# A dense layer worked as seven products: VectorE's and ScalarE's work in a pair of tiles put in another order, and the next tokens' columns prepared one step per pair

## The chip, the cores and the metric

The kernel runs on one core of a Trainium2 chip. The metric is the device time of one execution in microseconds (us). Three executions were timed, and one more was profiled; the rows below come from that one.

## The reference, cut to what matters

Three layers follow each other: attention, a routed layer that sends each token to one of eight experts, and a dense layer. The change touches the dense layer alone, and the hand-over to it.

```python
def _moe2_ref(x, w_in, w_out):          # x: 1792 x 768, w_in: 768 x 2048, w_out: 2048 x 768
    h = x @ w_in
    alpha = 1.0
    g = np.where(h > 0.0, h, alpha * (np.exp(np.minimum(h, 0.0)) - 1.0))
    return (g @ w_out).astype(np.float32)
```

## The kernel before, in words

All products are in 32-bit precision, made of rounded operands: a matrix `w` is split into a high part (a ScalarE cast) and a low part (a VectorE subtraction, `w` minus the high part), and a product takes three matmuls: high by high, high by low, low by high. `split` does this (L1440 the cast, L1441 the subtraction), for columns of `w_in` and for rows of `w_out`.

The 1792 tokens of the dense layer are 14 tiles of 128, worked in four blocks: blocks 0, 1 and 2 of four tiles (512 tokens), block 3 of two. The 2048 middle features are 16 tiles `f` of 128. Blocks 0 and 3 take one `f` at a time: `up` (18 matmuls over 512 or 256 tokens, L1487 to L1489), the curve (`curve`), and later `down`, which adds the tile's share to the output sums: for each of the token tiles six matmuls (L1519), three into 512 and three into 256 columns.

Blocks 1 and 2 take the features in eight pairs (`pair_step`) and get the pair's two `up` products from seven smaller ones instead of eight (`part(o, w, x, i)`, nine matmuls each over 256 tokens, L1540 to L1544). Here they are called P0 to P6 by their `i`; the order on TensorE is P1, P0, P3, P6, P2, P5, P4. They need, ready ahead of time:

- seven prepared forms of the tokens' columns, high and low (`x7`). For the next block they are made during this one: `rows_in` fetches a tile of rows, `columns_in` transposes it on TensorE (three matmuls for each of two halves, L145) and lets ScalarE copy it to a work buffer (L1376), `plain` makes the first three forms and then the four differences (L1395), `mixed` the other four forms (L1387, L1388).
- prepared forms of the pair's `w_in` columns: `a1` (P1, P0), `ss` (P3, P6, P2, P5) and `a2` (P4), split anew for the pair after this one while this one runs; and `sums` (L1463 to L1466, four VectorE operations) for the pair after that.

There are two PSUM banks for the parts, X and Y, each of 512 columns. P1 writes the right half of X, P0, P6, P5 and P4 the left half, P3 and P2 the left half of Y. Between them ScalarE copies (`p1`, `u2`, `p5`) and VectorE adds (L1599, L1612, L1614) put the pair's two products `h[0]` and `h[1]` together in SBUF. P6 may start when L1599 has read X.

The curve is, for a 128x512 tile: two ScalarE activations (L1496, L1497), a VectorE operation that gives `m` (L1498), a ScalarE cast `gh` (L1501) and a VectorE subtraction `gl` (L1502). `down` for feature tile `f` needs `gh`, `gl` and the split rows of `w_out`, `woh` and `wol`. In blocks 1 and 2 the `down` of a pair runs within the next pair: here D0 to D3 are its four token tiles for the pair's even feature tile, and E0 to E3 those for the odd one. After a block's last tile `finish` copies the output sums to the buffers `raw_t` (L1552), and POOL scatters them to the output (L1556).

The order of TensorE's, VectorE's and ScalarE's instructions is that of the code: each of the three works its list strictly one after the other. DMA loads of `w_in` and `w_out` (`refill`) are issued by SyncE's queue, which keeps up to five of each ahead.

Of the kernel before, what the change touches and what calls it, by code (L numbers as in the profile page):

```python
# [23 lines left out]
P = 128  # L24
# [70 lines left out]
def build(nc, tc, a):  # L95
# [3 lines left out]
    with ExitStack() as top:  # L99
# [1210 lines left out]
        with ExitStack() as st:  # L1310
# [20 lines left out]

            xr_t = [four(b0p.tile([P, WCH], F32, name="xr0")), four(raw_t[1])]

# [32 lines left out]
            def columns_in(bi, k, g, nxt, bank):  # L1366

                if not 0 <= k < blocks[bi][1]:
                    return
                t, r = turn_of(bi, k), rows_tile(k)  # L1370
                pt = bank.rearrange("p (c n) -> p c n", c=4)[:, :3]
                for j in range(3):
                    cc = 3 * g + j
                    flip(pt[:, j], r[:, cc * P : (cc + 1) * P])
                if seven[bi]:
                    nc.scalar.copy(xr_t[bi > 1][:, 2 * (t // 2) + g], pt)  # L1376
                    if (t // 2, g) == (1, 1):
                        plain(bi, nxt, t % 2)
                    return
                xh, xl = nxt  # L1380
                o = (slice(None), slice(3 * g, 3 * g + 3), slice(t * P, (t + 1) * P))
                nc.scalar.copy(xh[o], pt)
                nc.vector.tensor_sub(xl[o], pt, xh[o])
# [6 lines left out]
            def plain(bi, nxt, t):  # L1390
                r = xr_t[bi > 1]
                halves_in(nxt, slice(0, 2), r[:, :2], t)
                halves_in(nxt, slice(2, 3), r[:, 3:], t)
                for o, m, n in ((0, 2, 0), (2, 3, 2), (3, 3, 0), (1, 1, 3)):
                    nc.vector.tensor_sub(r[:, o], r[:, m], r[:, n])  # L1395

            def mixed(bi, nxt, t):
                r = xr_t[bi > 1]
                for o in (slice(0, 2), slice(2, 4)):
                    halves_in(nxt, slice(o.start + 3, o.stop + 3), r[:, o], t)  # L1400
# [90 lines left out]

            def curve(n, ph):
                m = gp.tile([P, TB * P], F32, name="m", bufs=1)
                gh = gp.tile([P, TB * P], F32R, name="gh")
                gl = gp.tile([P, TB * P], F32R, name="gl")
                nc.scalar.activation(m[:, :n], ph[:, :n], AF.Relu, scale=-1.0)  # L1496
                nc.scalar.activation(m[:, :n], m[:, :n], AF.Exp, scale=-1.0)  # L1497
                nc.vector.scalar_tensor_tensor(  # L1498
                    m[:, :n], m[:, :n], -1.0, ph[:, :n], op0=ALU.add, op1=ALU.max
                )  # L1500
                nc.scalar.copy(gh[:, :n], m[:, :n])  # L1501
                nc.vector.tensor_sub(gl[:, :n], m[:, :n], gh[:, :n])  # L1502
                return gh, gl

            def regions(acc, t):
# [77 lines left out]

            def pair_step(bi, p, x, pend, nxt):
                n = TB * P
# [13 lines left out]
                nc.vector.tensor_add(h[0][:, :HT], xr, p1)  # L1599
                if pairs:  # L1600
                    split_first(*after)
                    w_next = None
# [34 lines left out]

# [8 lines left out]
            nxt = None  # L1646
            pend = []
            for bi, (t0, nt) in enumerate(blocks):
                ahead_ = bi + 1 < len(blocks)
                if seven[bi]:  # L1650
                    for p in range(KF2 // 2):
                        if p == 3:
# [6 lines left out]
                        pend, w_in = pair_step(bi, p, xs, pend, nxt)  # L1659
                    xs = nxt  # L1660
                    continue
                for f in range(KF2):
# [11 lines left out]
                    ph = up(nt * P, [xs], *w_in) if bi or f else acc_t[1]  # L1674
                    w_in = w_next
                    if f + 1 == KF2 and ahead_:
                        split_sums(0)
                        split_sums(1)
                        split_last(bi + 1, 0)
                    g = curve(nt * P, ph)  # L1680
                    if ahead_:
                        turn, half = divmod(f - 6, 2)
                        if half == 0:
                            rows_in(bi + 1, turn)
                        turn, half = divmod(f - 7, 2)
                        if f == 7:
                            nxt = x_tiles(bi + 1)
                        if turn in (2, 4) and half == 0:
                            mixed(bi + 1, nxt, turn // 2 - 1)
                        if turn >= 0:  # L1690
                            columns_in(bi + 1, turn, half, nxt, next(halfway))
                    if bi == 0:
                        w2 = split_out(bi, f)
                    if due:
                        narrow_wide(due, 1)
                    if w2 is None:
                        run_down(pend[:TB])
                        pend = pend[TB:]
                        w2 = split_out(bi, f)
# [49 lines left out]
```

## Time and profile before

| | |
|---|---|
| three timed executions | 937.79, 938.77 (median), 940.61 us |
| the profiled execution's own time | 939.29 us |
| its span, first to last instruction | 937.5 us |
| attention and routed layer | 0 to about 403 us |
| dense layer, block 0 | about 403 to 546.3 us |
| blocks 1 and 2 (the pairs) | 546.3 to 856.4 us |
| block 3 and the last stores | 856.4 to 937.5 us |

The borders are read from TensorE's instructions: the first part at 546.29 us, the first `up` matmul of block 3 at 856.41 us. The span and the 1.8 us around it make the profiled execution's own time, which is 0.5 us above the median.

### The profile page before, as it was taken

How to read it: one execution, taken by the hardware profiler on the slowest of the kernel's cores; microseconds unless marked ns; L12 is line 12 of the kernel's file. 1: busy time of each engine (PE TensorE's matmuls, PEld its weight loads, DVE VectorE, ACT ScalarE, POOL GpSimd, SP SyncE). 2: the span in 40 equal slices, each digit the busy share in tenths (PEclk: the TensorE clock that was granted, in tenths of full speed). 3: DMA queues.
4: the chain of work that ended last, by engine and by line, in shares of the span. 5: the costliest groups of instructions: out<-in, count | busy, mean ns of one | idle time of the engine just before them, and what ended most of it. 6: DMA issues, size and time to landing. Idle time of an engine off the chain costs nothing.

```text
span 937.5 us, 15343 instructions
## 1 busy us (share of the span) xinstructions
PE 869.8 (93%) x5620; PEld 728.5 (78%) x5620; DVE 641.2 (68%) x1036; ACT 524.6 (56%) x796; POOL 82.2 (9%) x79
## 2 busy tenths in 40 slices
PE   9899999999998989999999976998888898999998
PEld 5444555989997878888887776887878788889997
DVE  5778786975664658858888876666565666564664
ACT  7677765534554548645455544554445455554664
POOL 1000001122010124510000001000000100000100
PEclk9999999999999999999999997999889999999999
DMA  9798867899461769478654734232222333223640
GB/s 326 260 320 310 306 232 253 290 400 378 168 237 56 269 245 398 155 265 275 208 159 127 265 105 148 85 119 85 85 85 68 134 103 101 73 97 100 237 153 34
DMA packets 64203, 180.83 MB, mean 193 GB/s; under 512 B 8010, under 2 KB 12234, under 8 KB 64098
## 3 DMA queue, kind: packets, MB, share of 16 engines
q1 hardware_dynamic: 59474, 160.27, 49.8%
q0 software_dynamic: 4480, 19.01, 5.9%
q8 instruction: 59, 0.97, 0.4%
q14 instruction: 46, 0.38, 0.1%
q10 hardware_dynamic: 144, 0.20, 0.1%
HBM read 152.58 MB, written 29.89 MB: 195 GB/s over the span
## 4 chain that ended last, share of the span: by engine, by line
PE 33%; DVE 12%; ACT 9%; issue 3%; DVEq 0%; ACTq 0%
PE acc L1519 7%; PE pt L1519 7%; PE acc L1540 3%; PE acc L1544 3%; PE acc L1543 3%; PE acc L1487 3%; PE acc L1489 3%; PE acc L1488 3%; DVE m L1498 2%; DVE wol L1441 2%; ACT m L1497 2%; ACT gh L1501 2%; ACT m L1496 2%; ACT woh L1440 1%; DVE wi L1464 1%
## 5 line engine op out<-in xcount | busy, mean ns | idle before, releaser
L594 DVE TENSOR_TENSOR wlo<-raw,whi 128x1536 fp32r<-128x1536 f32 x64 | 111.6, 1761 | 31.3 <-ACT whi L592 26.1
L253 ACT ACTIVATE at<-ps,bias 128x896 f32<-128x896 f32 x96 | 82.6, 916 | 39.1 <-PE ps L300 36.1
L592 ACT CAST whi<-raw 128x1536 fp32r<-128x1536 f32 x64 | 93.7, 1480 | 15.4 <-PE acc L603 9.0
L1519 PE MATMUL acc<-wol,gh 128*128 128x256 f32 x320 | 101.0, 316 | 0.0
L1519 PE MATMUL acc<-woh,gh 128*128 128x256 f32 x320 | 100.9, 315 | 0.0
L1519 PE MATMUL acc<-woh,gl 128*128 128x256 f32 x320 | 100.6, 314 | 0.0
L1540 PE MATMUL acc<-x,ss 128*128 128x256 f32 x192 | 61.6, 321 | 40.3 <-DVE h L1599 40.3
L601 PE MATMUL acc<-whi,both 128*128 128x384 f32 (+1 forms) x236 | 85.1, 361 | 4.3 <-issue 2.7
L602 PE MATMUL acc<-wlo,both 128*128 128x384 f32 (+1 forms) x236 | 83.4, 354 | 0.6 <-DVE wlo L594 0.6
L603 PE MATMUL acc<-whi,both 128*128 128x384 f32 (+1 forms) x236 | 83.2, 352 | 0.0
L1540 PEld LDWEIGHTS acc<-x,ss 128*128 128x128 f32 x192 | 42.4, 221 | 43.4 <-DVE h L1599 43.3
L1501 ACT CAST gh<-m 128x512 fp32r<-128x512 f32 (+1 forms) x64 | 36.3, 567 | 59.6 <-DVE m L1498 59.6
L1519 PEld LDWEIGHTS acc<-woh,gh 128*128 128x128 f32 x320 | 60.3, 188 | 10.1
L1502 DVE TENSOR_TENSOR gl<-m,gh 128x512 fp32r<-128x512 f32 (+1 forms) x64 | 40.0, 626 | 40.5 <-ACT gh L1501 39.8
L1519 PEld LDWEIGHTS acc<-wol,gh 128*128 128x128 f32 x320 | 60.3, 188 | 9.3
L1441 DVE TENSOR_TENSOR wol<-wor,woh 128x768 fp32r<-128x768 f32 x64 | 61.0, 954 | 7.9 <-ACT woh L1440 7.1
L1441 DVE TENSOR_TENSOR a<-wir,a 128x768 fp32r<-128x768 f32 (+1 forms) x47 | 38.4, 817 | 37.3 <-ACT a L1440 36.7
L1519 PEld LDWEIGHTS acc<-woh,gl 128*128 128x128 f32 x320 | 60.1, 188 | 4.3
L274 PE MATMUL po<-at,vt 128*64 128x448 f32 (+1 forms) x300 | 59.4, 532 | 2.4 <-DVE xT L305 2.4
L1543 PE MATMUL acc<-x,ss 128*128 128x256 f32 x192 | 59.2, 308 | 0.0
L1544 PE MATMUL acc<-x,ss 128*128 128x256 f32 x192 | 59.0, 307 | 0.0
L1440 ACT CAST woh<-wor 128x768 fp32r<-128x768 f32 x64 | 53.3, 833 | 2.8 <-PE acc L1519 2.8
(325 smaller groups left out, 2337.9 us busy)
## 6 DMA issues: line engine op xcount, KB each, us to landing
raw<-in_w SPq DMA_DIRECT2D x132, 384.0 KB
wor<-wo_d SPq DMA_DIRECT2D x60, 384.0 KB
wir<-wi_d SPq DMA_DIRECT2D x58, 384.0 KB
raw<-in_wi SPq DMA_DIRECT2D x9, 768.0 KB
raw<-in_wo SPq DMA_DIRECT2D x9, 768.0 KB
raw<-in_wi SPq DMA_DIRECT2D x14, 384.0 KB
raw<-in_wo SPq DMA_DIRECT2D x14, 384.0 KB
qr<-in_q SPq DMA_DIRECT2D x11, 448.0 KB
```

The costliest lines, as they stand in the source:

```text
L253: nc.scalar.activation(out, ps, AF.Sigmoid, bias=bias, scale=QK_SCALE)
L592: nc.scalar.copy(w_hi, raw)
L594: nc.vector.tensor_sub(w_lo, raw, w_hi)
L601: nc.tensor.matmul(o, a_hi, b_hi, start=first, stop=False)
L602: nc.tensor.matmul(o, a_hi, b_lo, start=False, stop=False)
L603: nc.tensor.matmul(o, a_lo, b_hi, start=False, stop=last)
L1440: nc.scalar.copy(pair[0], raw)
L1441: nc.vector.tensor_sub(pair[1], raw, pair[0])
L1519: nc.tensor.matmul(o, a, b, start=(clears and f == 0 and k_ == 0), stop=(f == KF2 - 1 and k_ == 2), skip_group_check=True,)
L1540: nc.tensor.matmul(o, a, b, start=(start and cc == 0), stop=False, skip_group_check=True)
L1543: nc.tensor.matmul(o, a, c, start=False, stop=False, skip_group_check=True)
L1544: nc.tensor.matmul(o, al[:, cc], b, start=False, stop=(cc == 2), skip_group_check=True)
```

## The change

No instruction of VectorE, ScalarE or TensorE in these blocks is added or taken away: the lists are put in another order, and one work buffer becomes two for block 2's columns.

1. The curve is cut into `rise` (to `m`) and `parts_of` (`gh`, `gl`). In a pair, the curve of `h[0]` now comes right behind the adds that make it, and ahead of P4; that of `h[1]` right behind P4's copy.
2. `sums`, which came at the end of a pair, now comes in the middle, behind the curve of `h[0]`.
3. The split of the odd `w_out` rows, which ended a pair, is put off to the middle of the next pair (`late`).
4. On TensorE, D0 now runs between P3 and P6, then D1 and D2, P4, D3 and E0 to E3. Before, D0 and D1 stood behind P5, then P4 and the other six.
5. The next tokens' columns: in blocks 1 and 2 the transposes come at pairs 1 to 4 (before: 3 to 6), and `plain`, `differences` and `mixed` are steps of their own at the end of pairs 2 to 7, one a pair (before: `plain` with the differences in pairs 4 and 6, `mixed` in pairs 5 and 7). For block 2 the work buffers are `raw_t[1]` and `raw_t[0]`, in place of `raw_t[1]` alone.
6. In block 0 the columns are made at feature tiles 3 to 6 and 10 to 13 (before: 7 to 14), and the steps at 7, 8, 9, 13, 14 and 15 (before: 10, 11, 14 and 15). At the last feature tile, the preparation of the first pair moves behind the curve.

```diff
-            xr_t = [four(b0p.tile([P, WCH], F32, name="xr0")), four(raw_t[1])]
+            xr_t = [[four(b0p.tile([P, WCH], F32, name="xr0"))] * 2, [four(raw_t[j]) for j in (1, 0)]]
...
-                    nc.scalar.copy(xr_t[bi > 1][:, 2 * (t // 2) + g], pt)
-                    if (t // 2, g) == (1, 1):
-                        plain(bi, nxt, t % 2)
+                    nc.scalar.copy(xr_t[bi > 1][t % 2][:, 2 * (t // 2) + g], pt)
...
-            def pair_step(bi, p, x, pend, nxt):
+            def pair_step(bi, p, x, pend, late, nxt):
...
-                rows_in(bi + 1, p - 2)
+                rows_in(bi + 1, p)
...
                 part(yl, w_s[0], x, 3, True)
                 nc.scalar.copy(p5, yl)
+                run_down(pend[:1])
                 part(xl, w_s[1], x, 6)
...
                 nc.vector.tensor_add(h[1][:, HT:], xl, p5)
+                m0 = rise(n, h[0])
                 if pairs:
                     split_sums(1)
-                run_down(pend[:2])
+                g0 = parts_of(n, m0)
+                pend2 = late() if late else []
+                if pairs and seven[later_[0]]:
+                    sums(*later_)
+                run_down(pend[1:3])
                 part(xl, a2, x, 4)
                 nc.scalar.copy(h[1][:, :HT], xl)
                 if pairs:
                     split_last(*after)
-                k = p - 3
-                if seven[bi + 1] and p in (5, 7):
-                    mixed(bi + 1, nxt, (p - 5) // 2)
-                columns_in(bi + 1, k, 0, nxt, Y)
-                g0 = curve(n, h[0])
-                run_down(pend[2:4])
-                columns_in(bi + 1, k, 1, nxt, X)
+                columns_in(bi + 1, p - 1, 0, nxt, Y)
+                m1 = rise(n, h[1])
+                run_down(pend[3:])
+                columns_in(bi + 1, p - 1, 1, nxt, X)
                 w20 = split_out(bi, 2 * p)
-                g1 = curve(n, h[1])
-                run_down(pend[4:])
-                if pairs and seven[later_[0]]:
-                    sums(*later_)
-                w21 = split_out(bi, 2 * p + 1)
+                g1 = parts_of(n, m1)
+                run_down(pend2)
+                if seven[bi + 1]:
+                    for j, todo in enumerate((plain, differences, mixed)):
+                        for t in range(2):
+                            if p == 2 + 3 * t + j:
+                                todo(bi + 1, nxt, t)
                 refill()
-                return tiles_of(bi, 2 * p, g0, w20) + tiles_of(bi, 2 * p + 1, g1, w21), w_next
+
+                def rest_of():
+                    return tiles_of(bi, 2 * p + 1, g1, split_out(bi, 2 * p + 1))
+
+                return tiles_of(bi, 2 * p, g0, w20), rest_of, w_next
```

Three places show what moved. The first is VectorE's list in a pair of block 2, before, from the split of `a2` to the add that opens the next pair (L1599). `h_15291` and `h_15292` are `h[0]` and `h[1]`, `acc_1907` is X, `a_11803` the low part of `a2`; `wi_1827` and `sraw` take the sums.

```order
L1441 TENSOR_TENSOR a_11803<-wir,a_11802 128x384
L1498 SCALAR_TENSOR_TENSOR m<-m,h_15291 128x512
L1502 TENSOR_TENSOR gl<-m,gh 128x512
L1441 TENSOR_TENSOR wol<-wor,woh 128x768
L1498 SCALAR_TENSOR_TENSOR m<-m,h_15292 128x512
L1502 TENSOR_TENSOR gl<-m,gh 128x512
L1463 TENSOR_TENSOR wi_1827<-wir 128x384
L1464 TENSOR_TENSOR wi_1827<-wi_1827,wir 128x384
L1465 TENSOR_TENSOR sraw<-wir,wi_1827 128x384
L1466 TENSOR_TENSOR sraw<-wir 128x384
L1441 TENSOR_TENSOR wol<-wor,woh 128x768
L1599 TENSOR_TENSOR h_15458<-acc_1907,p_15460 128x256
```

The same engine and stretch in the changed kernel, from the low part of the last `ss` to the add that opens the next pair, which is L1606 there.

```order
L1442 TENSOR_TENSOR ss_11805<-sraw,ss_11804 128x768
L1506 TENSOR_TENSOR gl<-m,gh 128x512
L1442 TENSOR_TENSOR wol<-wor,woh 128x768
L1464 TENSOR_TENSOR wi_1827<-wir 128x384
L1465 TENSOR_TENSOR wi_1827<-wi_1827,wir 128x384
L1466 TENSOR_TENSOR sraw<-wir,wi_1827 128x384
L1467 TENSOR_TENSOR sraw<-wir 128x384
L1442 TENSOR_TENSOR a_11803<-wir,a_11802 128x384
L1497 SCALAR_TENSOR_TENSOR m<-m,h_15286 128x512
L1442 TENSOR_TENSOR wol<-wor,woh 128x768
L1506 TENSOR_TENSOR gl<-m,gh 128x512
L1606 TENSOR_TENSOR h_15452<-acc_1907,p_15454 128x256
```

The four sums and the odd `wol` stood right ahead of the next pair's first add; now they stand in the middle of the pair, ahead of `m` of `h[1]`, and between the pair's last `gl` and that add nothing is left.

The second place is TensorE's matmuls from P3 to P6 in a pair of block 2, before (`acc_1908` is Y, `acc_1907` X).

```order
L1540 MATMUL acc_1908<-x_13524,ss_11804 128x256
L1543 MATMUL acc_1908<-x_13525,ss_11804 128x256
L1544 MATMUL acc_1908<-x_13524,ss_11805 128x256
L1540 MATMUL acc_1907<-x_13524,ss_11804 128x256
L1543 MATMUL acc_1907<-x_13525,ss_11804 128x256
L1544 MATMUL acc_1907<-x_13524,ss_11805 128x256
```

The same place in the changed kernel; `pt_1905` and `acc_1911` are the output sums of token tile 0.

```order
L1550 MATMUL acc_1908<-x_13185,ss_11804 128x256
L1551 MATMUL acc_1908<-x_13184,ss_11805 128x256
L1526 MATMUL pt_1905<-woh,gh 128x512
L1526 MATMUL pt_1905<-wol,gh 128x512
L1526 MATMUL pt_1905<-woh,gl 128x512
L1526 MATMUL acc_1911<-woh,gh 128x256
L1526 MATMUL acc_1911<-wol,gh 128x256
L1526 MATMUL acc_1911<-woh,gl 128x256
L1547 MATMUL acc_1907<-x_13184,ss_11804 128x256
L1550 MATMUL acc_1907<-x_13185,ss_11804 128x256
```

D0, six matmuls, now stands between the last matmul of P3 and the first of P6.

The third place is ScalarE's list at the first half-column of block 2 that is copied to the work buffer (`raw_121` is `raw_t[1]`; what an instruction waits for stands behind it, DMASW4 being one of POOL's transfers). Before, in pair 3 of block 1:

```order
L1619 COPY h_13527<-acc_1907 128x256 [waits PE_49]
L1440 CAST a_11802<-wir 128x384 [waits DMAHW1_49]
L1376 COPY raw_121<-acc_1908 128x384 [waits DMASW4_49,DVE_49,PE_49]
L1496 ACTIVATE m<-h_13526 128x512 [waits Activation_49]
L1497 ACTIVATE m<-m 128x512 [waits Activation_49]
L1501 CAST gh<-m 128x512 [waits DVE_49]
```

In the changed kernel, in pair 1 of block 1:

```order
L1632 COPY h_13187<-acc_1907 128x256 [waits PE_49]
L1441 CAST a_11802<-wir 128x384 [waits DMAHW2_49]
L1376 COPY raw_121<-acc_1908 128x384 [waits DMASW4_49,PE_49]
L1495 ACTIVATE m<-h_13187 128x512 [waits DVE_49,Activation_49]
L1496 ACTIVATE m<-m 128x512 [waits Activation_49]
L1376 COPY raw_121<-acc_1907 128x384 [waits PE_49]
L1441 CAST woh<-wor 128x768 [waits DMAHW7_49]
L1505 CAST gh<-m 128x512 [waits DVE_49]
```

The copy waits for the same transfer, two pairs sooner, and `h[1]`'s curve and the split of `woh` stand behind it on the engine.

## Rows read from the trace of the kernel before

**Rows 1.** Busy PE, PEld, DVE, ACT, POOL; PEclk; DMA share, GB/s; blocks 1 and 2.

```profile
546.30:856.40 310.10, 269.81 (x1788) 250.37 (x1789) 190.90 (x295) 158.75 (x284) 10.49 (x10) 0.94 0.30 96
```

**Rows 2.** Waits of TensorE, 400 to 938 us: total, times, longest.

```profile
PE acc L1540 <- DVE h L1599: 40.3, 15, 7.4
PE acc L1540 <- DVE m L1498: 3.4, 1, 3.4
...
PE acc L1487 <- DVE m L1498: 1.3, 2, 0.9
PE pt L1519 <- DVE wol L1441: 1.1, 1, 1.1
```

**Rows 3.** Timeline of TensorE over one pair: start, duration, instruction, idle before.

```profile
592.32 0.38 PE L1540 MATMUL acc<-x,ss 128*128 128x256 f32 x1 [1.40 <-DVE h L1599]
...
597.75 0.28 PE L1540 MATMUL acc<-x,a 128*128 128x256 f32 x1
...
598.83 0.40 PE L1519 MATMUL acc<-woh,gh 128*128 128x512 f32 x1
...
599.88 0.40 PE L1519 MATMUL acc<-woh,gh 128*128 128x512 f32 x1
...
608.25 0.28 PE L1544 MATMUL acc<-x,ss 128*128 128x256 f32 x1
609.92 0.38 PE L1540 MATMUL acc<-x,ss 128*128 128x256 f32 x1 [1.39 <-DVE h L1599]
```

**Rows 4.** Timeline of TensorE after the longest wait.

```profile
572.27 0.58 PE L1540 MATMUL acc<-x,ss 128*128 128x256 f32 x1 [7.40 <-DVE h L1599]
...
577.56 0.41 PE L1540 MATMUL acc<-x,ss 128*128 128x256 f32 x1
```

**Rows 5.** Timeline of VectorE at the same pair's end.

```profile
606.46 0.55 DVE L1463 TENSOR_TENSOR wi<-wir 128x384 f32<-128x384 f32 x1
...
608.58 0.95 DVE L1441 TENSOR_TENSOR wol<-wor,woh 128x768 fp32r<-128x768 f32 x1
609.45 0.42 DVE L1599 TENSOR_TENSOR h<-acc,p 128x256 f32<-128x256 f32 x1
```

**Rows 6.** Timeline of ScalarE at that place.

```profile
607.49 0.37 ACT L1598 COPY p<-acc 128x256 f32<-128x256 f32 x1 [0.94 <-PE acc L1544]
```

**Rows 7.** VectorE's groups by shape, 546 to 856 us: total, mean ns, idle before.

```profile
L1441 DVE TENSOR_TENSOR wol<-wor,woh 128x768 fp32r<-128x768 f32 x32 | 30.5, 953 | 1.3 <-ACT woh L1440 0.8
...
L1498 DVE SCALAR_TENSOR_TENSOR m<-m,h 128x512 f32<-128x512 f32 x32 | 22.1, 691 | 18.8 <-ACT m L1497 18.7
...
L1465 DVE TENSOR_TENSOR sraw<-wir,wi 128x384 f32<-128x384 f32 x15 | 8.4, 558 | 0.5
...
L1395 DVE TENSOR_TENSOR raw<-raw 128x384 f32<-128x384 f32 x8 | 4.4, 556 | 0.2
L1552 DVE COPY raw<-pt 128x512 f32<-128x512 f32 x4 | 2.6, 681 | 0.0
```

**Rows 8.** ScalarE's groups by shape, 546 to 856 us.

```profile
L1440 ACT CAST woh<-wor 128x768 fp32r<-128x768 f32 x32 | 26.7, 834 | 0.0
L1496 ACT ACTIVATE m<-h 128x512 f32<-128x512 f32 x32 | 20.3, 635 | 0.2
```

**Rows 9.** Timeline of TensorE: three transposes and the next matmul.

```profile
616.44 0.49 PE L145 MATMUL acc<-cst,xg 128*128 128x128 f32 x3
616.68 0.48 PE L1519 MATMUL acc<-woh,gh 128*128 128x512 f32 x1
```

**Rows 10.** Timeline of POOL: first and third scatter of block 0's output.

```profile
565.09 1.00 POOL L1556 DMA_INDIRECT out<-raw,order  x1 [34.49 <-ACT woh L1440]
...
573.12 0.97 POOL L1556 DMA_INDIRECT out<-raw,order  x1 [2.91 <-DVE a L1441]
```

**Rows 11.** These scatters' time to landing, 540 to 640 us.

```profile
DMA to landing us min/median/max: 3.0/3.1/3.2
```

**Rows 12.** Fetched rows of tokens (384 KB each), time to landing, 440 to 860 us.

```profile
DMA to landing us min/median/max: 3.9/4.4/6.7
```

More of the change, by code (lines that the diff above doesn't have):

```diff
@@ L1390, in plain, with differences @@
             def plain(bi, nxt, t):
-                r = xr_t[bi > 1]
+                r = xr_t[bi > 1][t]
                 halves_in(nxt, slice(0, 2), r[:, :2], t)
                 halves_in(nxt, slice(2, 3), r[:, 3:], t)
+            def differences(bi, nxt, t):
+                r = xr_t[bi > 1][t]
                 for o, m, n in ((0, 2, 0), (2, 3, 2), (3, 3, 0), (1, 1, 3)):
@@ L1397, in mixed @@
             def mixed(bi, nxt, t):
-                r = xr_t[bi > 1]
+                r = xr_t[bi > 1][t]
                 for o in (slice(0, 2), slice(2, 4)):
@@ L1490, in up, with rise @@
                 return ph
-            def curve(n, ph):
+            def rise(n, ph):
                 m = gp.tile([P, TB * P], F32, name="m", bufs=1)
-                gh = gp.tile([P, TB * P], F32R, name="gh")
-                gl = gp.tile([P, TB * P], F32R, name="gl")
                 nc.scalar.activation(m[:, :n], ph[:, :n], AF.Relu, scale=-1.0)
@@ L1500, in curve, with parts_of @@
                 )
+                return m
+            def parts_of(n, m):
+                gh = gp.tile([P, TB * P], F32R, name="gh")
+                gl = gp.tile([P, TB * P], F32R, name="gl")
                 nc.scalar.copy(gh[:, :n], m[:, :n])
@@ L1503, in curve @@
                 return gh, gl
+            def curve(n, ph):
+                return parts_of(n, rise(n, ph))
             def regions(acc, t):
@@ L1599, in pair_step @@
                 nc.vector.tensor_add(h[0][:, :HT], xr, p1)
+                w_next = None
                 if pairs:
                     split_first(*after)
-                    w_next = None
                 else:
@@ L1646, in build @@
             nxt = None
-            pend = []
+            pend, late = [], None
             for bi, (t0, nt) in enumerate(blocks):
@@ L1651, in build @@
                     for p in range(KF2 // 2):
-                        if p == 3:
+                        if p == 1:
                             nxt = x_tiles(bi + 1)
@@ L1658, in build @@
                                 ]
-                        pend, w_in = pair_step(bi, p, xs, pend, nxt)
+                        pend, late, w_in = pair_step(bi, p, xs, pend, late, nxt)
                     xs = nxt
@@ L1675, in build @@
                     w_in = w_next
+                    g = curve(nt * P, ph)
+                    if ahead_:
+                        for k in range(4):
+                            if f == (2, 4, 7, 9)[k]:
+                                rows_in(bi + 1, k)
+                            for half in range(2):
+                                if f == (3, 5, 10, 12)[k] + half:
+                                    if (k, half) == (0, 0):
+                                        nxt = x_tiles(bi + 1)
+                                    columns_in(bi + 1, k, half, nxt, next(halfway))
+                        for when, todo, t in (
+                            (7, plain, 0), (8, differences, 0), (9, mixed, 0),
+                            (13, plain, 1), (14, differences, 1),
+                        ):
+                            if f == when:
+                                todo(bi + 1, nxt, t)
+                    if bi == 0:
+                        w2 = split_out(bi, f)
                     if f + 1 == KF2 and ahead_:
                         split_sums(0)
+                        mixed(bi + 1, nxt, 1)
                         split_sums(1)
                         split_last(bi + 1, 0)
[L1680 to L1693, printed above, removed]
                     if due:
                         narrow_wide(due, 1)
-                    if w2 is None:
-                        run_down(pend[:TB])
-                        pend = pend[TB:]
+                    if late:
+                        run_down(pend)
+                        pend, late = late(), None
                         w2 = split_out(bi, f)
```

## Prediction

> **What bounds the kernel now.** I read the stretches first, then TensorE's waits, then one pair instruction by instruction. The pairs of blocks 1 and 2 take 310.1 us [rows 1]; TensorE is at work in 269.8 of them, VectorE in 190.9, ScalarE in 158.8, so no engine is full, and TensorE is the nearest. It waits 40.3 us in 15 waits, one at the same place in every pair but the last: L1540 after VectorE's L1599 [rows 2], which is P6 behind the pair's first add. Near the hand-over from block 0 there are 3.4, 1.3 and 1.1 us more [rows 2]. That is the first loss.
>
> The second is the clock. The granted clock is 0.94 in this stretch [rows 1]. After the wait of 7.40 us, 24 steps of one matmul take 5.29 us, 0.22 each [rows 4]; elsewhere nine matmuls of a part take 1.08 us (597.75 to 598.83) and a token tile of `down` 1.05 us [rows 3]. So TensorE runs at its lower level, 1.2 GHz, after long waits, and at 2.4 GHz otherwise; after the waits of 1.4 us the usual pace is back at once [rows 3]. To size it: a pair is 7 x 1.08 + 8 x 1.05 = 15.96 us of matmuls (592.32 to 608.25 agrees). Sixteen pairs are 255.4; the first lacks the four odd tiles (-4.2), and 12 half-columns of transposes at 0.32 (0.24 to the next matmul, which takes some 0.08 longer [rows 9]) add 3.8. That is 255.0, and 269.8 is spent: 14.8 us go to the lower clock and to restarts.
>
> Why P6 waits: the copy `p1` ended at 607.86 [rows 6], but the add began only at 609.45, because the four sums (from 606.46) and the odd `wol` (608.58) stood ahead of it on VectorE [rows 5]. The data was ready 1.6 us before the adder. Pairs that carry `plain`, the differences or `mixed` have more ahead of it, and wait longer.
>
> **The change, part by part.** No work is added, so every cost is a wait. I walk a pair without columns in the new order, time zero at P6's first matmul.
>
> TensorE, if it never waits: P6 to 1.08, P2 2.16, P5 3.24, D1 and D2 5.34, P4 6.42, D3 7.47, E0 to E3 11.67, then P1, P0, P3 14.91 and D0 15.96. A part's result is there 0.16 later (a matmul lasts 0.28, the next starts after 0.12 [rows 3]). Durations are those of [rows 5 to 8]; the next instruction on VectorE starts some 0.08 before the end of the one ahead (608.58 + 0.95 against 609.45), unless it needs its result.
>
> - ScalarE: `u2` to 1.65, high part of `ss` to 2.4, then, behind the adds, the two activations (0.63 each) to 5.1, `ss` again to 5.8, `gh` 6.5, odd `woh` 7.2.
> - VectorE: low part of `ss` to 3.4, the adds 3.8 and 4.1, `m` 5.8, `ss` 6.8, `gl` 7.4, odd `wol` 8.3, the sums 10.4, `a2` 10.9, `m` of `h[1]` 11.5, even `wol` 12.3, `gl` 12.9.
>
> Two things follow. First, the next pair's add finds VectorE free at 12.9. It waits for P0 (14.4 with the wait below) and `p1`, runs from 15.0 to 15.5, and P6 wants X at 16.6: 1.1 us early, where it is 1.6 us late now. A step at the end of a pair takes at most 4 x 0.56 = 2.3 us (the differences, [rows 7]), so VectorE is free at 15.2 and the margin 0.9. **The 40.3 us go.**
>
> Second, E0 starts at 7.47 and its second matmul, at 7.7, reads the odd `wol`, ready at 8.3: **a new wait of 0.6 us.** In the six pairs with columns two half-columns (0.6) stand ahead of E0 and leave 0.1. With 8 pairs at 0.6 and 6 at 0.1, it costs 5.4. The bounds: nothing, if the split comes 0.6 sooner; 1.5, the size of today's wait in a plain pair [rows 3], for eight pairs 12 us.
>
> *Hand-over from block 0.* Between `m` of the last tile and the first add of pair 0, VectorE now has `gl` 0.69, `wol` 0.95, `ss` 0.95, two low parts of columns 1.9 (priced as `wol`), `ss` 0.95, `a2` 0.56, four sums 2.2: 8.2 us, 7.5 with the overlaps, and it starts late by up to 1. TensorE has P1, P0, P3, D0, 4.3 us. So P3 and P6 wait some 4.2 together, P1 and the steps of block 0 about 1.0: 5.2 in place of the 5.8 of [rows 2]. **-0.6**, bounds -5.8 and +3.
>
> *Pair 1 of block 1.* Pair 0 has no odd tiles, and `finish` puts four copies (4 x 0.6, [rows 7]) ahead of the even `wol`, which is ready at 12.3 - 0.9 (no odd `wol`) + 2.4 = 13.8; D0's second matmul wants it at 15.96 - 4.2 - 0.8 = 10.9. **+2.9**; bounds 0 and 5.
>
> *The first column copy* now comes in pair 1 and waits for the third scatter (the third place of the order above), which lands 573.12 + 0.97 + 3.1 - 565.09 = 12.1 us after the first is issued [rows 10, 11]. In the walk the first scatter goes out at about 12, some 0.8 after its copy, so the third lands at 24; the copy is wanted at 7.9 in a pair that begins at 14.7, at 22.6. ScalarE stands 1.5 us; `m` of `h[1]` has 1.8 of cover, since the sums keep VectorE until 10.9 and ScalarE is done at 9.1. I take **0**. Without that cover, the wait goes through to TensorE; with one scatter more to wait for (4 us) it would cost some 4, the upper bound.
>
> *Columns of block 3*, with the low parts in pairs 1 and 2 of block 2: **+0.3**, bounds 0 and 3.
>
> *The clock.* With no wait above 2.9 us but the ones at the hand-over and in pair 1, I keep 2 of the 14.8: **-12.8**; bounds -14.8 and -5 (if waits in the first pairs hold it down).
>
> The sum: -40.3 + 5.4 - 0.6 + 2.9 + 0.3 - 12.8 = -45.1, on the profiled execution's 939.3: 894.2. That execution is 0.5 above the median, so against the median of the runs it is 893.7. I forecast **894 us**.
>
> A rule speaks against the first term. The trace shows the add late and the bank ready [rows 5, 6]. The Trainium skill, page "Perfetto Trace Analysis", section "Optimization Strategy", says that a gap which repeats on the engine that should be saturated can mean too few buffers for the next tile; the change adds no PSUM bank, so by that rule the gaps would stay, and the sum would be near 911. The row here gives the 1.6 us to VectorE's queue, and I follow it.
>
> **The rivals.**
>
> *X is the limit* (the second PSUM bank is what is missing). Then all 15 waits stay at today's plain 1.5: 22.5 in place of none. For it: P6 writes the half of X that L1599 does not read and still waits [rows 2]. Against it: `p1` and the add take 0.9 us after P0, and P3 with D0 now cover 2.1. Time 894 + 22.5 - 5.4 = 911. Chance 0.07.
>
> *The odd `wol` is later than walked*, by 1 us in every pair, ScalarE having nine instructions in a row ahead of it: 14 more, 908. Chance 0.10.
>
> *The steps of block 1 do not fit the margin of 0.9*: six pairs lose 1 us, the scatter 4, the clock 3 more: 907. Chance 0.08.
>
> *The walk is too careful*: its new waits vanish (5.4 + 2.9), since instructions overlap more than assumed: 886. Chance 0.13.
>
> *Slower: the sums wait for their load.* They run some 6 us earlier in a pair. The `w_in` tile they read is issued, at the latest, behind the even `wol` of the pair before (12.3), and wanted at 8.3 + 16.6 = 24.9: 12.6 us for a transfer that for as many bytes takes 4.4, at most 6.7 [rows 12]. Beyond 12.6 VectorE stands, and the add, with 1.1 of margin, is late by the rest. To lose the 45 us again, 14 pairs must each lose 3.2: a landing time of 17 us. At 18 it would be 948. Chance 0.02, with 0.02 that lesser delays leave no change.
>
> **How the numbers follow.** The forecast has 0.58, 888 to 900 with the small terms' bounds. The three slower rivals, 907 to 911, have 0.25, the quicker one 0.13. The range 882 to 912 takes in the four rivals on its edges and leaves out about 0.1 to 0.15, the sums of bounds on one side. A difference below 0.3% (2.8 us) can't be told from none here. Faster 0.96, same 0.02, slower 0.02.
>
> **What would show it.** Right: the waits of TensorE's parts for the first add are gone from block 1's second pair on; a plain pair takes about 16.6 us (17.6 now, 592.32 to 609.92); a wait of about 0.6 us of L1526's second matmul for `wol` stands in plain pairs; the stretch of the pairs takes about 269 us at a granted clock near 0.99; the pair-1 copy stands for a DMA. The prediction is wrong if the add still comes late, if E0 waits over 1 us, if VectorE waits for a load ahead of the sums, or if the clock stays below 0.97.

## The result, and the profile after

| | |
|---|---|
| before, four executions of the comparison | 937.79 to 940.61, median 938.63 us |
| changed, four executions | 892.40 to 895.69, **median 893.67 us** |
| changed to before | **0.952, 95% interval 0.9497 to 0.9543** |
| the changed kernel's profiled execution | 892.40 us, span 890.4 us |

894 us was forecast. The page of the changed kernel gives for the whole span each engine's busy time, and TensorE's granted clock in 40 slices:

```profile
PE 857.8 (96%) x5620; PEld 715.8 (80%) x5620; DVE 636.4 (71%) x1036; ACT 522.6 (59%) x796; POOL 78.2 (9%) x79
...
PEclk9999999999999999999999999999999999999999
```

The stretch of the 16 pairs, from the first matmul of P1 to the first `up` matmul of block 3 (columns as in [rows 1]):

```profile
540.00:809.32 269.32, 258.86 (x1789) 238.02 (x1790) 190.47 (x300) 159.69 (x288) 10.68 (x10) 0.99 0.35 112
```

It is 310.1 us long in [rows 1] and 269.3 here, 40.8 less; the forecast for it was 269 at a clock of 0.99. The work is the same: VectorE 190.9 and 190.5 us. TensorE stands 10.5 us in place of 40.3, and its own matmuls take 258.9 in place of 269.8. Waits of TensorE from 530 to 830 us, as in [rows 2]:

```profile
PE pt L1526 <- DVE wol L1442: 6.4, 9, 2.1
PE acc L1547 <- DVE h L1606: 2.4, 1, 2.4
PE acc L1547 <- DVE m L1497: 1.0, 1, 1.0
PE acc L1550 <- DVE x L1386: 0.9, 1, 0.9
PE acc L1547 <- ACT x L1385: 0.4, 1, 0.4
PE acc L1547 <- ACT raw L1376: 0.3, 1, 0.3
```

The 15 waits for the first add, now L1606, are one: pair 0, at the hand-over. What is new is the first row, nine waits of L1526's second matmul (`pt`) for a `wol`: eight are E0's for the odd half in plain pairs, 0.47 to 0.58 each; the longest, 2.09, is D0's for the even half in pair 1. One plain pair on TensorE, as in [rows 3]:

```profile
731.85 0.29 PE L1547 MATMUL acc<-x,ss 128*128 128x256 f32 x1
...
740.16 0.50 PE L1526 MATMUL pt<-wol,gh 128*128 128x512 f32 x1 [0.58 <-DVE wol L1442]
740.50 0.40 PE L1526 MATMUL pt<-woh,gl 128*128 128x512 f32 x1
...
748.36 0.29 PE L1547 MATMUL acc<-x,ss 128*128 128x256 f32 x1
```

P6 starts at 731.85 and again at 748.36: a pair takes 16.51 us (17.60 in [rows 3]), with one wait, of 0.58. VectorE in the same pair:

```profile
739.15 0.95 DVE L1442 TENSOR_TENSOR wol<-wor,woh 128x768 fp32r<-128x768 f32 x1
...
744.08 0.68 DVE L1506 TENSOR_TENSOR gl<-m,gh 128x512 fp32r<-128x512 f32 x1
746.89 0.42 DVE L1606 TENSOR_TENSOR h<-acc,p 128x256 f32<-128x256 f32 x1 [2.13 <-ACT p L1605]
```

Counted from 731.85, the odd `wol` ends at 8.25 (8.3 in the walk of the prediction), `gl`, the last of VectorE's list, at 12.91 (12.9), and the add starts at 15.04 (15.0). VectorE now stands 2.13 us before the add, and the add ends 1.05 before P6: the add waits for its data; the data no longer waits for VectorE. Last, the first column copy of pair 1, on ScalarE:

```profile
575.55 0.48 ACT L1376 COPY raw<-acc 128x384 f32<-128x384 f32 x1 [2.93 <-DMA out<-raw,order]
```

It stands 2.9 us for the scatter of block 0's output (the walk said 1.5), and 0.3 of that reaches TensorE, the last row of the waits.

### The profile page after: what moved, and what is told of

It reads as the page before. It is cut to its first block, busy times and chain, and to the rows that moved or that the text cites. A ratio compares the mean times of both kernels' runs of the same rounds, so it can differ in the third digit from the quotient of the medians.

```text
span 890.4 us, 15324 instructions
## 1 busy us (share of the span) xinstructions
PE 857.8 (96%) x5620; PEld 715.8 (80%) x5620; DVE 636.4 (71%) x1036; ACT 522.6 (59%) x796; POOL 78.2 (9%) x79
## 4 chain that ended last, share of the span: by engine, by line
PE 37%; DVE 11%; ACT 5%; issue 2%; DMA 0%; ACTq 0%; DVEq 0%
PE acc L1526 11%; PE pt L1526 8%; PE acc L1547 3%; PE acc L1551 3%; PE acc L1550 3%; PE acc L1488 3%; PE acc L1490 3%; PE acc L1489 3%; DVE ss L1442 2%; DVE wol L1442 2%; ACT ss L1441 2%; ACT m L1495 1%; ACT m L1496 1%; DVE raw L165 1%; DVE m L1497 1%
## 5 line engine op out<-in xcount | busy, mean ns | idle before, releaser
L1526 PE MATMUL acc<-wol,gh 128*128 128x256 f32 x320 | 100.9, 315 | 0.0
L1526 PE MATMUL acc<-woh,gh 128*128 128x256 f32 x320 | 100.8, 315 | 0.0
L1526 PE MATMUL acc<-woh,gl 128*128 128x256 f32 x320 | 100.5, 314 | 0.0
L1526 PEld LDWEIGHTS acc<-woh,gh 128*128 128x128 f32 x320 | 60.3, 188 | 10.1
L1526 PEld LDWEIGHTS acc<-wol,gh 128*128 128x128 f32 x320 | 60.3, 188 | 9.4
L1526 PEld LDWEIGHTS acc<-woh,gl 128*128 128x128 f32 x320 | 60.1, 188 | 4.2
L1526 PE MATMUL pt<-wol,gh 128*128 128x512 f32 x128 | 52.2, 408 | 6.4 <-DVE wol L1442 6.4
L1547 PE MATMUL acc<-x,ss 128*128 128x256 f32 x192 | 54.8, 285 | 2.8 <-DVE h L1606 2.4
L1550 PE MATMUL acc<-x,ss 128*128 128x256 f32 x192 | 54.5, 284 | 0.9 <-DVE x L1386 0.9
L1551 PE MATMUL acc<-x,ss 128*128 128x256 f32 x192 | 54.3, 283 | 0.0
L1506 DVE TENSOR_TENSOR gl<-m,gh 128x512 fp32r<-128x512 f32 (+1 forms) x64 | 39.7, 621 | 19.3 <-ACT gh L1505 19.3
L1526 PE MATMUL pt<-woh,gh 128*128 128x512 f32 x128 | 52.3, 408 | 0.0
```

What stands on the lines that cost most here:

```text
L1526: nc.tensor.matmul(o, a, b, start=(clears and f == 0 and k_ == 0), stop=(f == KF2 - 1 and k_ == 2), skip_group_check=True,)
L1547: nc.tensor.matmul(o, a, b, start=(start and cc == 0), stop=False, skip_group_check=True)
L1550: nc.tensor.matmul(o, a, c, start=False, stop=False, skip_group_check=True)
L1551: nc.tensor.matmul(o, al[:, cc], b, start=False, stop=(cc == 2), skip_group_check=True)
```

## The experiments

Each was timed in five or more rounds beside the kernel before, whose median was 937 to 941 us. "Idle" below is the length of the pairs' stretch, read as above, less TensorE's busy time in it.

### Four parts of the change, each undone by itself

Parts 1 to 4 of the change are undone here. The earlier place of the next tokens' columns and their steps (parts 5 and 6) were never undone by themselves, and no two parts were undone together.

**The sums back at the pair's end.**

```diff
-                if pairs and seven[later_[0]]:
-                    sums(*later_)
                 run_down(pend[1:3])
...
                 run_down(pend2)
+                if pairs and seven[later_[0]]:
+                    sums(*later_)
```

> The changed kernel with the four sums put back at the end of the pair, behind the steps' other work; everything else as changed. Theory (each first add has margin to spare, and the sums are only one of the pieces that give it): with the early curve, the odd split put off and D0 ahead of P6, VectorE is through at about 12.9 of a pair with the sums as well, since they move from one place of the same pair to a later one and nothing else is behind them. The plain pairs stay at 16.5 us, only pairs with a step wait (about 2 us in pair 1 of block 1, 0.6 in a pair with the differences): 895 us, +1. Rival (the sums' move is what made the kernel faster): the first add is late again by 1.6 us in every plain pair and more in others, the granted clock falls to about 0.94: 915 us or more.

Measured: 893.5 us, ratio 0.9522 (0.9495 to 0.9549), the changed kernel's own ratio. Its waits:

```profile
PE pt L1526 <- DVE wol L1442: 5.8, 9, 1.5
PE acc L1547 <- DVE h L1606: 4.4, 2, 2.4
```

The add is late in pairs 0 and 1 (2.40 and 1.97) and in no other. The rival is out: with the rest of the change there, the sums' place doesn't matter.

**The curve of `h[0]` back behind P4's copy.**

```diff
-                m0 = rise(n, h[0])
                 if pairs:
                     split_sums(1)
-                g0 = parts_of(n, m0)
...
                 columns_in(bi + 1, p - 1, 0, nxt, Y)
+                g0 = parts_of(n, rise(n, h[0]))
                 m1 = rise(n, h[1])
```

> The changed kernel with the whole curve of h[0] put back behind the copy of P4 and the first half-column, as before the change. Theory (VectorE and ScalarE must be early at the end of the pair, and the early curve is what moves two activations, m, gh and gl ahead): the adds come late by 0.7 to 1.2 us in some pairs with steps, transposes and P1 wait for a column's copy by 0.7 to 2.8 us, while E0 stops waiting for the odd low half: +10 us, 904. Rival (the sums' place alone decides): no wait returns, 894 or a little under.

Measured: 900.0 us, 0.9567 (0.9547 to 0.9587). Of the four it is the only part whose undoing makes the kernel slower, by 6 us and not 10. The profiled execution took 909.0 us and the other five 898.7 to 900.7, so the waits below are those of a longer execution; which of them the others had isn't shown. Its largest waits:

```profile
PE acc L1547 <- ACT raw L1376: 4.7, 4, 3.7
PE acc L1547 <- DVE h L1606: 4.4, 4, 2.4
PE pt L1526 <- ACT woh L1441: 3.0, 1, 3.0
PE acc L1547 <- DVE x L1381: 2.4, 2, 1.2
```

They are spread over several places; the add's share is 4.4 us, 2.4 of it in pair 0. The longest is that of P1 in pair 2. ScalarE's timeline ahead of it:

```profile
584.61 0.48 ACT L1376 COPY raw<-acc 128x384 f32<-128x384 f32 x1 [3.22 <-DMA out<-raw,order]
...
589.62 0.46 ACT L1376 COPY raw<-acc 128x384 f32<-128x384 f32 x1
```

and P1 on TensorE:

```profile
590.13 0.58 PE L1547 MATMUL acc<-x,a 128*128 128x256 f32 x1 [3.66 <-ACT raw L1376]
```

The copy of the first half-column stands 3.22 for the scatter; then five instructions of the two curves come, with waits between them, and only then the copy of the second half, for which P1 waits in bank X. In the changed kernel two activations stand there, and a stand of 2.93 costs TensorE 0.3. That is the case that the prediction named for this copy: "Without that cover, the wait goes through to TensorE". Its price of some 4 us was for another cause, one scatter more to wait for; here the copy's own stand is twice the 1.5 of the walk.

**D0 back behind P5.**

```diff
                 nc.scalar.copy(p5, yl)
-                run_down(pend[:1])
...
-                run_down(pend[1:3])
+                run_down(pend[:3])
```

> The changed kernel with D0 put back behind P5, so that P6 follows P3 at once, and D0, D1 and D2 follow P5. Theory (the add is early, so D0 ahead of P6 covers nothing in most pairs, and its place only brings E0 1.05 us nearer to the odd low half): the 0.6 us waits at E0 go, the wait in pair 1 too, and P6 waits 3.0 to 3.6 us in the first two pairs only: 889 us, -4 to -5. Rival (bank X is the limit, D0 is the cover for the copy p1 and the add): P6 waits about 1 us in every pair, 15 times, and with the 5 us of E0 gained the kernel takes 904 us or more.

Measured: 891.0 us, 0.9473 (0.9444 to 0.9501), 2.7 below the changed kernel with intervals that overlap: not slower. Its only wait for the add:

```profile
PE acc L1547 <- DVE h L1606: 6.2, 2, 3.4
```

P6 waits in pairs 0 and 1 (3.44 and 2.71) and in none of the other 14 by more than 0.1 us, and E0 doesn't wait at all. In a plain pair the add, and P6 behind the last matmul of P3:

```profile
764.90 0.42 DVE L1606 TENSOR_TENSOR h<-acc,p 128x256 f32<-128x256 f32 x1 [2.27 <-ACT p L1605]
```

```profile
765.20 0.28 PE L1551 MATMUL acc<-x,ss 128*128 128x256 f32 x1
765.38 0.39 PE L1547 MATMUL acc<-x,ss 128*128 128x256 f32 x1
765.60 0.28 PE L1550 MATMUL acc<-x,ss 128*128 128x256 f32 x1
```

P6 comes 0.18 after P3's last matmul and its own second 0.22 after that, where the usual step is 0.12: 0.16 in all, and the pair takes 15.76 us in place of the 15.60 of plain pairs without any wait (pairs 12 to 14 of the next run). So even when P6 follows P3 at once, bank X costs a plain pair at most 0.16 us and not the 1 us of the rival.

**The odd split back at its own pair's end.**

```diff
+                w21 = split_out(bi, 2 * p + 1)
+
                 def rest_of():
-                    return tiles_of(bi, 2 * p + 1, g1, split_out(bi, 2 * p + 1))
+                    return tiles_of(bi, 2 * p + 1, g1, w21)
```

> The changed kernel with the split of the odd out-weights put back at the end of its own pair, everything else as changed. Theory (this part of the change is not needed for the first add, whose margin is longer than 0.95 us, and it is what makes E0 wait): E0's waits go, 5 us; a pair with a step waits 0.5 to 1 us at P6 or P3, 2 us in all: 890.5 us, in a range of 889 to 892.5. Rival (the put-off split is one of the pieces that hold the add early): the add waits in the plain pairs too, 0.5 us or more each, 897 or more.

Measured: 888.5 us, 0.9465 (0.9441 to 0.9488): 5 us faster than the changed kernel, at the lower end of what was expected. The waits:

```profile
PE acc L1547 <- DVE h L1606: 3.1, 2, 2.4
PE pt L1526 <- DVE wol L1442: 2.1, 1, 2.1
```

E0's eight waits are gone, and the add is late only in pairs 0 (2.4) and 1 (0.7). This part of the change costs 5 us and saves nothing.

### One part alone, on the kernel before

**The sums alone:** the two lines of `sums` moved from the end of the pair to ahead of `run_down(pend[:2])`.

> The kernel before with one edit of the change alone: the four sums moved from the pair's end to behind the second split of ss. Theory (the first add waits for what stands ahead of it on VectorE, and the sums are 2.2 us of that): the plain pairs, whose add is 1.6 us late, stop waiting, eight or nine of the 15 waits go, 2 to 5 us stay in the pairs with plain, differences or mixed and in the first two: 26 us less of waits, and of the clock's 12.8 perhaps half: 907 us, in a range of 903 to 913. Rival (the sums only move the queue, since the curve of h[0] now stands behind them): the waits stay, 930 or more.

**The early curve alone:** `curve` cut into `rise` and `parts_of`, which stand around `split_sums(1)` as in the changed kernel.

> The kernel before with one other edit alone: the curve of h[0] taken apart and moved ahead of P4, as in the changed kernel; sums, odd split, D0 and the columns' steps stay as before. Theory (the waits are one queue's, and any piece that leaves the end of the pair shortens them): plain pairs wait 0.3 us in place of 1.4, the others 2 to 5: 21 us less of waits, some 5 of the clock: 913 us, in a range of 908 to 918. This edit and the sums' move, each alone, together take more than the whole change does, 26 + 21 of the waits' 40, since in a plain pair either of them is enough. Rival (the sums' move alone makes the gain): 930 or more.

Measured: the sums alone 905.6 us, 0.9653 (0.9622 to 0.9684); the curve alone 912.7 us, 0.9728 (0.9695 to 0.976). The row of the first add, with the sums moved:

```profile
PE acc L1540 <- DVE h L1599: 16.4, 7, 5.4
```

and with the curve moved:

```profile
PE acc L1546 <- DVE h L1605: 19.1, 13, 4.9
```

Both expectations hold. The sums, 2.2 us of VectorE, free every plain pair (7 waits are left: pairs 0 and 1 of block 1, four pairs behind its steps, and pair 1 of block 2); the curve only shortens the waits. Beside the kernel before of the same rounds (937.7 us), the first gains 32 us by itself and the second 25, where the whole change gains 45. What the two gain together, without the rest, was not run.

### The wait at E0, and a faster version

**The odd split right behind `m` of `h[0]`.**

```diff
                 m0 = rise(n, h[0])
+                pend2 = late() if late else []
                 if pairs:
                     split_sums(1)
                 g0 = parts_of(n, m0)
-                pend2 = late() if late else []
```

> The changed kernel with the split of the odd out-weights right behind m of h[0], ahead of the second split of ss and of gh and gl: one line moved. Theory (E0's second matmul waits 0.6 us for the odd low half because it stands behind ss and gl on VectorE): the eight waits of about 0.55 us go, nothing else is late since gl is read a matmul later and ss only by the next pair, 889 us, -5. Rival (something else than VectorE's order holds E0, or the place of the wait moves): the waits go from wol to gl or to the add of the next pair, 893 to 895.

Measured: 887.6 us, 0.9436 (0.9414 to 0.9457), against 0.9497 to 0.9543 of the changed kernel: faster. Two of its waits:

```profile
PE acc L1547 <- DVE h L1606: 2.4, 1, 2.4
PE pt L1526 <- DVE wol L1442: 1.6, 1, 1.6
```

The eight waits are gone, and the one for `wol` that is left is D0's in pair 1. So VectorE's order made them.

**And the second pair's sums out of the hand-over.**

```diff
-                    if ahead_ and f + 2 >= KF2:
-                        sums(bi + 1, f + 2 - KF2)
+                    if ahead_ and f + 2 == KF2:
+                        sums(bi + 1, 0)
...
                 if pairs:
+                    if (bi, p) == (1, 0):
+                        sums(*after)
                     split_first(*after)
```

> The version with the odd split right behind m of h[0], and the sums of block 1's second pair computed in its first pair, behind the first add, instead of at the end of block 0. Theory (in the hand-over these sums are four operations between the last low part and the first add, and P6 waits 2.4 us): that wait falls to 0.4 or nothing and nothing waits for the sums, which are wanted 3 us later: 2 us less than 887.6, 885.5, and the best of all. Rival (something else than the sums holds the first add, or the sums are then late for the second pair's split of ss): 887.5 to 889.

Measured: 885.5 us, 0.9445 (0.9413 to 0.9476). The add's wait:

```profile
PE acc L1547 <- DVE h L1606: 0.3, 1, 0.3
```

It falls from 2.4 to 0.3; a new one of 0.8 for `gh` appears in pair 1, and D0's there grows from 1.6 to 2.1. The pairs take 260.98 us (262.52 with the split alone). The two versions' times can't be told apart; both are faster than the changed kernel.

### The margin and the price of the clock

**More work for VectorE at the end of each pair**, into a tile that nothing reads by then:

```diff
                 run_down(pend2)
+                for _ in range(12):
+                    nc.vector.tensor_sub(u2, p5, p5)
```

> The changed kernel with 12 more VectorE operations of 128x256 at the end of each pair, some 0.3 us apart, 3.6 us in all, which write a scratch tile that nothing reads; the output is the same. It puts waits back without moving anything. Theory (margin at the add 2.1 and at P6 1.1 in a plain pair, the odd low half's 0.6 besides; in pairs with a step 0.9): plain pairs wait 0.2 us, pairs with a step 1.6 to 2.6, pair 1 3.6, some 22 us in all; and the clock goes down with the waits as it did before, where 40 us of waits cost 12.8: some 6 more: 919 us, granted clock of the pairs about 0.96. Rival on the margin (bank X, not VectorE, holds P6 just as it is): every pair waits the whole 3.6, 945 or more. Rival on the clock (waits below 3 us cost nothing of it): granted clock 0.99, 914.

Measured: 956.4 us, 1.0192 (1.0158 to 1.0225). Neither number held, since the load was wrong: the twelve took 5.47 us, 0.456 each, not 3.6. The pairs' stretch:

```profile
543.16:872.99 329.83, 280.68 (x1788) 259.17 (x1789) 263.77 (x482) 161.78 (x288) 10.72 (x10) 0.91 0.30 92
```

P6 waits 1.7 to 2.1 us in the plain pairs of block 2. By the changed kernel's rows VectorE stands 2.13 before the add and P6 comes 1.05 after its end, so of 5.47 some 2.3 should arrive: the margin is there; that it is a little larger may come from slower matmuls, which cover more, but that is not shown. The run with eight has the load that was meant:

> The changed kernel with 8 more VectorE operations a pair. In the run with 12 they took 0.456 us each (12 in 5.47), not the 0.3 that was assumed, so that run's load was 5.5 us and not 3.6; this one has the 3.65 us. Theory as there (margin 2.1 at the add and 1.1 at P6 in a plain pair, 0.6 more by E0's wait, 0.9 with a step): plain pairs wait 0.4 us, pairs with a step 1.4 to 2.8, pair 1 3.8: 25 us of waits, and 0.2 of that again for the clock: 924 us, in a range of 918 to 930, clock of the pairs 0.95. Rival (no margin): 3.65 in every pair, 950 or more.

Measured: 920.8 us, 0.9821 (0.9808 to 0.9834). Waits and stretch:

```profile
PE acc L1547 <- DVE h L1606: 18.8, 12, 3.4
```

```profile
540.22:834.86 294.64, 266.89 (x1789) 244.65 (x1789) 237.86 (x422) 160.83 (x288) 10.60 (x10) 0.97 0.33 103
```

The time lies in the range, and the plain pairs of block 2 wait 0.2 us (one 1.0), others up to 3.4; the clock is 0.97 and not 0.95.

**P3 a second time in the wait.** TensorE gets work where it stands:

```diff
+                part(Y[:, HT:], w_s[0], x, 3, True)
                 part(xl, w_s[1], x, 6)
```

> The kernel before with nine more matmuls in each pair: P3 is computed a second time into the half of bank Y that nothing uses then, ahead of P6, so in the wait for the first add. The output is the same; no wait is taken away, TensorE only stands for 1.1 us less of each. Theory (the granted clock falls because TensorE stands, so the clock's 14.8 us are a price of the waits): 14 waits shrink by 1.08 each, the idle time of the pairs from 40 to 25, the matmuls of the pairs lose some 9 us to the clock instead of 14, and the pair without a wait pays 1.1: 4 us faster than before with more work, 934, granted clock 0.96. Rival (the clock goes by something else, the work in a stretch or its position): 1 to 3 us slower than before, clock 0.94.

> The kernel with 12 more VectorE operations a pair, with P3 computed two more times into the unused half of bank Y ahead of P6, 2.16 us of matmuls in waits of 2.4 to 5.2. Theory (as for the fill of the kernel before): the pairs' idle time falls from 49 to some 17, the clock from 0.91 to 0.97, their other matmuls take about 263 instead of 281, and the time is 956.5 less some 14: 942. Rival (clock by something else): 956 or more, clock 0.91.

One statement of the first is wrong, for both: the output does not stay the same. The Trainium skill, "PSUM — Partial Sum Buffer", section "The four PSUM rules", says that the start of a sum clears the marks of its whole bank; by that, P2 overwrites P3's sum in Y in place of adding to it. The trace can't show it. The instructions and their sizes are as told, and their times are used here; the values of `h[0]`'s right half are not.

Measured on the kernel before: 934.1 us, 0.9972 (0.9954 to 0.9991): with 144 matmuls more, it is not slower but 0.3% faster. The stretch:

```profile
544.94:849.48 304.54, 281.64 (x1932) 261.07 (x1933) 190.62 (x295) 158.88 (x284) 10.00 (x10) 0.97 0.32 98
```

Idle is 22.9 us in place of 40.3, most of it now ahead of the added matmuls, which wait for the copy `p5` out of the same bank:

```profile
PE acc L1540 <- ACT p L1606: 18.0, 16, 5.4
```

The added matmuls, 144 at the usual 0.12, are 17.3 of the 281.6; the others take 264.4 in place of 269.8. The granted clock is 0.97 in place of 0.94, and four pairs (0, 1, 7 and 9) are below 1.00 in place of seven. So these 5.4 us, some 3 if the medians are taken in place of the two profiled executions, were a price of standing, unless the changed values have a part in it, which was not tried.

With the twelve operations the second fill failed as an experiment: 983.4 us, 1.0481 (1.0466 to 1.0496). Its first row of waits:

```profile
PE acc L1547 <- ACT p L1613: 34.2, 14, 4.6
```

The fill waited for the copy `p5` here too, and that copy for the added VectorE operations, which read `p5`. So the fill came behind the wait and not into it, and P6 was later by its length. It tells nothing of the clock.

## Why the prediction was right

**The step that carries it held.** The add was late because of what stood ahead of it on VectorE. Two edits to that queue alone shorten or remove its waits without touching a bank, D0's return leaves 14 pairs without one of more than 0.1 us, and loads put back on VectorE bring the waits back less the margin. The page "Perfetto Trace Analysis" of the Trainium skill, section "Optimization Strategy", reads such repeated gaps as a possible lack of buffers. By it the time was to be 911 us; here the gaps went with no PSUM bank added. Of the other rivals, the odd `wol` is late by 0.47 to 0.58 us and not by 1 more, no pair with a step waits for the add, and in the pairs VectorE waits for no transfer, so the sums' load isn't late.

**The terms,** forecast and then read from the two profiled executions:

| term | forecast | measured |
|---|---|---|
| the add's waits (pair 0's new one stands under the hand-over) | -40.3 | -40.3 |
| E0 on the odd `wol` | +5.4 | +4.3 (8 plain pairs, 0.5 to 0.6; none in pairs with columns) |
| hand-over from block 0 | -0.6 (5.2) | -0.7 (5.1: 0.4, 1.0, 0.4, 0.9 and 2.4) |
| D0 of pair 1 | +2.9 | +2.1 |
| column copy behind the scatter | 0 | +0.3 |
| columns of block 3 | +0.3 | 0 (no wait of its own) |
| matmuls at the lower clock, restarts | -12.8 | -10.9 (269.8 to 258.9) |

The measured ones make -45.2; the profiled executions differ by 46.9. The rest, 1.7, lies ahead of the pairs, where the first P1 comes between 537.8 and 545.3 us in the profiles of the changed kernel and its variants, whose code up to block 0 is the same.

**Sizes that were off.** The matmuls take 3.9 us over the 255.0 of the sum, not 2, and the clock is the smaller part of it. Pair 0 takes 14.05 us of matmuls at a granted clock of 0.90, and 12.62 at 1.00 in the version with its sums moved: 1.4. The rest is E0's, at a clock of 1.00: a plain pair of block 2 takes 16.50 us with a wait of 0.57 and 15.60 without one, so the wait costs 0.9; in the plain pair above, the matmul after it comes 0.34 before the next in place of 0.23. By the pairs' lengths E0's eight waits cost some 6.7 us, 4.3 of them as waits; so E0's term, 5.4, was too low, though its waits were walked 1.1 too high, and the version that takes them away is 6 us faster. ScalarE's stand for the scatter was nearly double, and by the run with the curve put back the early curve kept most of it from TensorE. That the time came within 1 us of the forecast is luck: these errors of 1 to 2 us cancel, so that the sum is closer than its terms.

**What the prediction did not say** is which parts are needed. The experiments show that the change is more than enough: VectorE ends its list 2.1 us before the add, so sums or D0, each alone, can go back for nothing, and the odd split's new place is a loss of 5 us. Of the four parts only the early curve is needed in the changed kernel, and, by its one profiled execution, less for the add than for the columns' copies and the even `woh`, which queue behind the curve on ScalarE. What the columns' new place and steps are worth stays open; with the sums alone on the kernel before, the four pairs behind the old steps still wait 7.6 us and pair 1 5.4.

## What to carry to other kernels

When an engine waits for another's instruction, compare the end of that instruction's last input with its start. If the input was ready earlier, look at what stands ahead of the instruction on its engine, move one such piece to where that engine stands idle, and stop once the instruction waits for its own input: a further move can make something else late, as the odd split did. Try each part of a reordering alone and undone, since parts that shorten the same wait don't add up (32 and 25 us here by themselves, 45 for the whole change). Price TensorE's waits at more than their length, by what the matmuls after them lose.

## What the runs showed of the hardware

What TensorE loses by standing, beyond the wait itself, has two parts, and the pairs show them one by one. Three pairs of the kernel before (the columns as in [rows 1]):

```profile
687.15:710.40 23.25, 18.64 (x113) 17.38 (x112) 14.90 (x23) 10.26 (x18) 0.00 (x0) 0.85 0.21 68
710.40:730.89 20.49, 17.47 (x113) 16.24 (x112) 12.18 (x19) 9.89 (x18) 0.00 (x0) 0.92 0.27 79
752.29:769.71 17.42, 15.87 (x113) 14.62 (x112) 10.99 (x18) 9.26 (x16) 0.00 (x0) 1.00 0.30 91
```

Here the pairs are counted from 0 to 15 through both blocks. All rows are of pairs without columns:

| kernel, pair | wait in it, us | its matmuls, us | granted clock |
|---|---|---|---|
| before, 7 | 4.61 | 18.64 | 0.85 |
| before, 9 | 3.94 | 17.46 | 0.92 |
| before, 8 | 3.02 | 17.47 | 0.92 |
| before, 10 | 1.55 | 15.87 | 1.00 |
| before, 15 | none | 15.76 | 1.00 |
| changed, 12 | 0.57 (E0) | 15.92 | 1.00 |
| changed, 15 | none | 15.60 | 1.00 |

The waits of 0.57 and 1.55 us leave the granted clock at 1.00 and cost 0.3 and 0.1 in the matmuls at their ends. After the waits of 3 us and more the clock of the pair is 0.85 to 0.92, a mean over time at 2.4 GHz and time at 1.2, and its matmuls take 1.6 to 2.8 us longer than those of pair 10. In the kernel before, seven pairs (0, 1 and 5 to 9) are below 1.00, in the changed one only pair 0, at 0.90. Between these lengths the wait alone doesn't decide: one of 2.63 left the clock at 1.00 (sums alone, pair 7), one of 2.04 took it to 0.91 (twelve more, pair 14). What does decide there is not shown.

Over the pairs' whole stretch, kernels with the same matmuls:

| kernel | TensorE idle, us | its matmuls, us | granted clock |
|---|---|---|---|
| early odd split, sums moved | 4.8 | 256.2 | 0.99 |
| early odd split | 6.5 | 256.0 | 0.99 |
| changed, odd split back | 6.5 | 256.8 | 0.99 |
| changed, D0 back | 7.5 | 258.6 | 0.98 |
| changed | 10.5 | 258.9 | 0.99 |
| changed, sums back | 11.6 | 260.0 | 0.99 |
| before, sums alone | 16.4 | 260.4 | 0.98 |
| changed, curve back (the execution of 909.0 us) | 18.7 | 262.2 | 0.98 |
| before, curve alone | 19.3 | 263.2 | 0.97 |
| eight more operations | 27.8 | 266.9 | 0.97 |
| before | 40.3 | 269.8 | 0.94 |
| twelve more operations | 49.2 | 280.7 | 0.91 |

From the changed kernel's row on, each microsecond in which TensorE stands goes with another 0.36 (sums alone) to 0.55 (twelve more) of matmul time against the first row. That is a mean over pairs of both kinds and no price of a single wait. The idle time alone doesn't order the rows: with D0 back it is 3 us less than in the changed kernel, but two long waits (3.44 and 2.71) put pairs 0 and 1 at 0.82 and 0.92, and in a plain pair of block 2 P6 loses 0.16.
